# Attention and two feed-forward blocks on one core: the strided masks' queue, raw weight buffers, and the constants of the kernel's planner

## The chip, the cores and the metric

The kernel runs on one core of a Trainium2 chip. The core has a matrix engine (TensorE, PE below; PEld is its weight load), a vector engine (VectorE, DVE), an activation engine (ScalarE, ACT), GpSimd (POOL) and a sync engine (SyncE, SP) that only issues DMAs. Time is device microseconds of one execution; three runs of the kernel before took 823.49, 823.75 and 825.63 us, median 823.75 us.

## The reference, cut to what matters

```python
# attention: 4 batches, 8 heads, 576 positions, 64 per head
scores = scale * np.matmul(q, k.transpose(0, 1, 3, 2))
mask_local   = (rel >= 0) & (rel < 32)                       # heads 0 to 3
mask_strided = (rel >= 0) & (pos_k % 32 == pos_q % 32)       # heads 4 to 7
scores = np.where(mask, scores, -1e9)
attn = softmax(scores)                                       # exp, sum + 1e-9, divide
x = np.matmul(attn, v)                                       # gathered to 2304 tokens x 512
# first feed-forward block
h = x @ w_in;  g = h * np.clip(h + 3.0, 0.0, 6.0) / 6.0;  x = g @ w_out      # 512 -> 2048 -> 512
# second
h = x @ w_in2; g = h * np.tanh(softplus(h));              out = g @ w_out2
```

## The kernel before

**Layout and precision.** The host reorders q, k and v by pairs of heads (4 pairs a batch: 0 and 1 local, 2 and 3 strided), and hands the weights over as 64-bit words. `unpack` loads one 128x512 half of a weight block (a tile `raw`, 512 KB, L793), turns it into float32 in `wa` by four or five DVE instructions, one of them on ACT for the first 20 tiles (the magnitude, L797; then L807, L811, L816, L822 or L830). `split` (L348, L776) writes a float32 tile as a rounded high part (a CAST, mostly on ACT) and a low part (a subtraction on DVE or POOL). A product of two such tiles is three matmuls (`mm3`, L1012 to L1014).

**Stages.** The first feed-forward block begins before attention has ended. Its first part takes four of sixteen blocks of the hidden width plainly, in five runs of tokens (512, 448, 512, 320, 512), while batches 1 to 3 go through attention. The rest of it and the whole second block take 384 tokens twice at a time by a seven-product (Strassen-like) scheme, whose sums and differences of weights (`difference`, L898), of x (L958) and of g (L1237, L1255) run on DVE or POOL, and whose results are added up on DVE (L1221, L1295).

**Attention of one pair** (`attend`): a group of 76 score matmuls (L609), three mask additions on DVE (L622), row maximum (L654), subtraction (L655, DVE or POOL), exp on ACT (L656), row sum (L657), a guard (L661 or L663), reciprocal (L666), multiplication (L667, DVE or POOL), six transposes on PE (L676, L678), copies of them out of PSUM (`pt`, L348), 72 value matmuls (L715), and two copies into `xs`. The first two pairs take the softmax in two halves of 320 and 256 columns. `load_pair` loads q and k of a pair (`qk`, 576 KB), the values (`v`, 432 KB and a small rest) and copies some of their rows (L575, on ACT mostly). The tiles of pairs 2 and 3 of batch 0 lie in the `xs` tiles, so their loads and copies read `xs<-in_qkv_dram`.

**Masks.** The local mask comes in one load (`mk`, L489). The strided one comes in seven small loads of rows of 64 floats (`mk_str`, `mk_odd`, L515), issued by ACT with a due time of 1000, and POOL or DVE then place parts of them (L532).

**Order.** Nothing is ordered by hand. `Plan` holds every operation with costs by engine, dependencies and a due time; `run` lays them out in time with the constants at the head of the file, takes for each engine the most urgent operation that can start soonest (within `SOON`), and, where an operation may run on several engines, the one that would end it first, after a `BIAS` for each. Where PE would be idle in the first 60 us it puts in matmuls on zeros (`fill`, L1382; 'fillers' below), whose result nobody reads. The order in which `run` laid them out is the order of each engine's instructions in the program; each engine takes its own strictly in that order, and an instruction waits for the semaphores of what it needs.

**DMA semaphores.** The DMAs of all queues take eight semaphores in turn (DMAHW0 to DMAHW7). A DMA whose semaphore is taken is issued only after the transfer eight DMAs before it has landed. The planner before does not count this.

**Buffers.** There are two `raw` tiles. The load of a third waits until the first has been decoded.

## Time and profile before

| what | value |
|---|---|
| three runs | 823.49, 823.75, 825.63 us |
| the profiled execution | 822.89 us |
| its span (first to last instruction) | 821.10 us |
| mean granted clock of TensorE | 0.997 of full |
| busy: PE, DVE, ACT, POOL | 808.3, 676.0, 447.2, 325.9 us |
| DMA | 182.31 MB, mean 222 GB/s |
| last PE instruction ends | 3.4 us before the end of the span |

The page gives one profiled execution. Its time (822.89 us) holds 1.79 us that lie outside the span, and is 0.86 us under the median of the three runs. PE busy includes the fillers, so a busy PE in the first 60 us is not always at work for the result. The idle time of an engine is put down to what ended it.

### The profile page before, as it was taken

Reading aid. Unit: us, or ns where it says so; the run is one execution under the profiler, and the core shown is the slowest. Engines: PE = TensorE matmul, PEld = TensorE weight load, DVE = VectorE, ACT = ScalarE, POOL = GpSimd, SP = SyncE. Lnnn points to the kernel's source line nnn. Section 1 sums busy time; section 2 is a strip of 40 time slices with the busy share of each in tenths; the row PEclk is TensorE's granted clock in tenths of the full one; section 3 lists DMA queues with packets and bytes.
Section 4 is the critical chain, followed back from the end, with each engine's and each line's share of the span. In section 5 each row is a group of like instructions: output and inputs, shape, how many; then the busy total and the mean of one; then the engine's idle time right before and its main releaser. Section 6 shows DMA issues by size and latency. Waiting matters only on the chain.

```text
span 821.1 us, 17043 instructions
## 1 busy us (share of the span) xinstructions
PE 808.3 (98%) x6650; PEld 771.0 (94%) x6650; DVE 676.0 (82%) x1238; ACT 447.2 (54%) x941; POOL 325.9 (40%) x324
## 2 busy tenths in 40 slices
PE   6999999999999999999999999999999999999998
PEld 3678888899999999999999999999999999999998
DVE  4888887898999857867889899776888999998766
ACT  2767767666654434434436568556555545545542
POOL 4443421412252314231424324422677456476223
PEclk9999999999999999999999999999999999999999
DMA  8786751477678866765866446665667667765732
GB/s 241 229 248 184 211 178 54 146 303 268 249 251 297 295 251 238 263 226 184 288 219 229 184 168 268 225 239 196 241 240 244 225 212 244 247 237 188 246 126 96
DMA packets 47588, 182.31 MB, mean 222 GB/s; under 512 B 6036, under 2 KB 15380, under 8 KB 47508
## 3 DMA queue, kind: packets, MB, share of 16 engines
q1 hardware_dynamic: 46848, 181.06, 64.0%
q8 instruction: 52, 0.85, 0.4%
q10 hardware_dynamic: 660, 0.16, 0.1%
q14 instruction: 28, 0.23, 0.1%
HBM read 138.74 MB, written 42.47 MB: 221 GB/s over the span
## 4 chain that ended last, share of the span: by engine, by line
PE 89%; DVE 4%; DMA 3%; ACT 1%; POOL 1%; issue 1%; ACTq 0%; SPq 0%; DVEq 0%
PE bank L1012 29%; PE bank L1013 28%; PE bank L1014 28%; PE bank L715 2%; DMA raw<-in_wts_dram 1%; PE bank L609 1%; DMA v<-in_qkv_dram 1%; PE bank L676 1%; DMA mk_str<-in_masks_dram 1%; POOL w L898 1%; PE bank L1382 0%; DMA qk<-in_qkv_dram 0%; DVE wa L816 0%; DVE xs L1295 0%; DVE wa L811 0%
## 5 line engine op out<-in xcount | busy, mean ns | idle before, releaser
L1012 PE MATMUL bank<-x,win 128*128 128x384 f32 (+3 forms) x668 | 227.8, 341 | 0.4 <-POOL win L776 0.2
L1013 PE MATMUL bank<-x,win 128*128 128x384 f32 (+3 forms) x668 | 226.2, 339 | 0.1
L1014 PE MATMUL bank<-x,win 128*128 128x384 f32 (+3 forms) x668 | 226.1, 338 | 0.0
L1012 PE MATMUL bank<-g,wout 128*128 128x384 f32 (+3 forms) x512 | 175.7, 343 | 0.0
L1013 PE MATMUL bank<-g,wout 128*128 128x384 f32 (+3 forms) x512 | 174.2, 340 | 1.1 <-DVE g L776 1.1
L1014 PE MATMUL bank<-g,wout 128*128 128x384 f32 (+3 forms) x512 | 174.0, 340 | 0.0
L1295 DVE TENSOR_TENSOR xs<-bank,xs 128x384 f32<-128x384 f32 x174 | 95.2, 552 | 49.5 <-PE bank L1014 48.3
L1012 PEld LDWEIGHTS bank<-x,win 128*128 128x128 f32 x668 | 125.4, 188 | 5.3 <-POOL win L776 1.4
L1013 PEld LDWEIGHTS bank<-x,win 128*128 128x128 f32 x668 | 125.4, 188 | 2.8 <-POOL x L776 0.5
L1014 PEld LDWEIGHTS bank<-x,win 128*128 128x128 f32 x668 | 125.4, 188 | 2.2
L1013 PEld LDWEIGHTS bank<-g,wout 128*128 128x128 f32 x512 | 96.1, 188 | 3.0 <-DVE g L776 1.1
L1014 PEld LDWEIGHTS bank<-g,wout 128*128 128x128 f32 x512 | 96.1, 188 | 2.3
L1012 PEld LDWEIGHTS bank<-g,wout 128*128 128x128 f32 x512 | 96.1, 188 | 2.0
L898 POOL TENSOR_TENSOR w<-w 128x256 f32<-128x256 f32 x80 | 68.2, 871 | 70.1 <-DVE w L830 69.0
L1013 PE MATMUL bank<-g_late,wout 128*128 128x384 f32 x204 | 68.1, 334 | 0.0
L1012 PE MATMUL bank<-g_late,wout 128*128 128x384 f32 x204 | 68.1, 334 | 0.0
L1014 PE MATMUL bank<-g_late,wout 128*128 128x384 f32 x204 | 68.1, 334 | 0.0
L776 POOL TENSOR_TENSOR x<-xs,x 128x512 fp32r<-128x512 f32 (+3 forms) x17 | 21.1, 1244 | 63.7 <-ACT x L348 52.9
L816 DVE SCALAR_TENSOR_TENSOR wa<-raw,wa 128x512 uint32<-128x512 uint32 x64 | 45.8, 723 | 0.3
L776 POOL TENSOR_TENSOR win<-w,win 128x256 fp32r<-128x256 f32 (+1 forms) x25 | 29.1, 1170 | 40.6 <-ACT win L348 34.9
L348 ACT CAST win<-w 128x512 fp32r<-128x512 f32 (+1 forms) x56 | 31.6, 567 | 22.8 <-DVE w L830 14.6
L348 ACT COPY u<-bank 128x384 f32<-128x384 f32 x42 | 20.2, 482 | 37.6 <-PE bank L1014 37.4
(139 smaller groups left out, 1481.6 us busy)
## 6 DMA issues: line engine op xcount, KB each, us to landing
x<-kept_s SPq DMA_DIRECT2D x60, 768.0 KB, 4.4
x<-kept_a SPq DMA_DIRECT2D x45, 768.0 KB, 4.6
raw<-in_wts_dram SPq DMA_DIRECT2D x64, 512.0 KB, 5.0
kept_s<-x SPq DMA_DIRECT2D x24, 768.0 KB, 3.4
kept_a<-x SPq DMA_DIRECT2D x18, 768.0 KB, 4.0
qk<-in_qkv_dram SPq DMA_DIRECT2D x14, 576.0 KB, 5.3
v<-in_qkv_dram SPq DMA_DIRECT2D x14, 432.0 KB, 5.0
keep<-y SPq DMA_DIRECT2D x24, 192.0 KB, 4.1
```

What stands on the lines that cost most here:

```text
L348: nc.scalar.copy(out, src)
L609: nc.tensor.matmul(banks[both[h].n][g * QN:(g + 1) * QN, slot * WK:(slot + 1) * WK], src.q[h * D:(h + 1) * D, n // 6, n % 2 * QN:(n % 2 + ...
L676: nc.tensor.transpose(banks[turned[0].n][:, j * P:(j + 1) * P], e[:, t:t + 2].rearrange("p s k -> p (s k)"), ident)
L715: nc.tensor.matmul(o[h * D:(h + 1) * D], src.v[rows, NB + others(local).index(n) if n in others(local) else i, h * D:(h + 1) * D], pt[rows ...
L776: lambda eng: engines[eng].tensor_tensor(lo(), src(), hi().bitcast(F32), ALU.subtract),
L816: lambda: nc.vector.scalar_tensor_tensor(ai, high, 0xC0000000, ai, ALU.bitwise_and, ALU.bitwise_or),
L898: lambda eng: engines[eng].tensor_tensor(of[out], of[x], of[y], ALU.subtract), [*on[x], *on[y]], lock=("dve", "pool"),
L1012: nc.tensor.matmul(o, low_w, high, start=first, stop=False, skip_group_check=True)
L1013: nc.tensor.matmul(o, high_w, low, start=False, stop=False, skip_group_check=True)
L1014: nc.tensor.matmul(o, high_w, high, start=False, stop=last, skip_group_check=True)
L1295: "dve", dve_ns(n), lambda: nc.vector.tensor_tensor(y(), src(), y(), ALU.add), [prev, y_sums[key]], due=due, frees=frees,
```

## The change

The seven loads of the strided masks go to the sync queue and get a due time of 14000. Three more `raw` tiles, allocated beside attention's, serve with the two old ones for the first eight weight loads; the end of attention's memory then waits for their decoding too. `run` now lets a DMA start only once the eighth before it has landed (`LANES`). And most constants of the planner get new values, which moves instructions on all engines. Over the whole program the order has 1356 DVE instructions after 1240 (116 more), POOL 204 after 329, ACT's 945 after 943 beside its DMAs, and 18 fillers of 512 columns after 17; of the 80 weight differences on POOL (L898) 54 go to DVE.

```diff
+N_RAW_MORE, RAW_EARLY = 3, 8
+LANES = 8
-START, FIRST_PACE = 42920, 3359
+START, FIRST_PACE = 40873, 3220
-MASKS_DUE = 1000
-SOON = 11
+MASKS_DUE = 14000
+SOON = 0
-BIAS = {"act": -305, "dve": 318, "pool": 0}
+BIAS = {"act": -834, "dve": 384, "pool": 290}
...
                     if e == "pe":
                         t += self.late(t, op)
+                    elif e == "dma" and len(landed) >= LANES:
+                        t = max(t, landed[-LANES])
...
+            if e == "dma":
+                landed.append(op.end + self.AFTER[e])
...
+    raw_t.extend(ap_.tile([P, DM], U64, name=f"raw_more{k}") for k in range(N_RAW_MORE))
...
-            return add("act", 430, lambda: nc.scalar.dma_start(to(rows), src), due=MASKS_DUE)
+            return add("dma", 400, lambda: nc.sync.dma_start(to(rows), src), due=MASKS_DUE)
...
-        raw, a = raw_t[n % N_RAW], wa_t[n % N_WA]
+        slot = n % (N_RAW + N_RAW_MORE) if n < RAW_EARLY else n % N_RAW
+        raw, a = raw_t[slot], wa_t[n % N_WA]
...
-        old = raw_ops[n - N_RAW] if n >= N_RAW else []
+        old = raw_last.get(slot, [])
...
+            if slot >= N_RAW:
+                closing.deps.append(o)
```

Line numbers of the kernel after are 5 to 11 higher than those of the kernel before (L609 becomes L615, L1012 becomes L1023).

**The sync queue at the start.** The rows are the DMAs that SP issues, in order, with the semaphores that each waits for. `mk` is the local mask, `qk0`, `qk1`, `xs0` and `xs1` hold q and k of pairs 0 to 3, `v0` and `v1` the values of pairs 0 and 1. Before:

```order
L489 DMA mk_139<-in_masks_dram 128x320
L547 DMA qk0_143<-in_qkv_dram 128x1152
L547 DMA qk1_144<-in_qkv_dram 128x1152
L547 DMA xs0_75<-in_qkv_dram 128x1152 [waits DMAHW2_49]
L559 DMA v0_145<-in_qkv_dram 96x1152 [waits DMAHW3_49]
L547 DMA xs1_76<-in_qkv_dram 128x1152 [waits DMAHW4_49]
L559 DMA v0_145<-in_qkv_dram 64x128 [waits DMAHW5_49]
L793 DMA raw0_79<-in_wts_dram 128x512 [waits DMAHW6_49]
L559 DMA v1_146<-in_qkv_dram 96x1152 [waits DMAHW7_49]
L559 DMA v1_146<-in_qkv_dram 64x128 [waits DMAHW0_49]
L559 DMA xs2_77<-in_qkv_dram 96x1152 [waits DMAHW1_49]
L793 DMA raw1_80<-in_wts_dram 128x512 [waits DMAHW2_49]
```

And now:

```order
L497 DMA mk_139<-in_masks_dram 128x320
L800 DMA raw0_79<-in_wts_dram 128x512
L553 DMA qk0_143<-in_qkv_dram 128x1152
L800 DMA raw1_80<-in_wts_dram 128x512
L553 DMA qk1_144<-in_qkv_dram 128x1152
L553 DMA xs0_75<-in_qkv_dram 128x1152
L523 DMA mk_str_141<-in_masks_dram 128x1x64 x2
L523 DMA mk_odd_142<-in_masks_dram 64x1x64 [waits DMAHW0_49]
...
L523 DMA mk_str_141<-in_masks_dram 64x1x64 [waits DMAHW4_49]
L565 DMA v0_145<-in_qkv_dram 96x1152 [waits DMAHW5_49]
L553 DMA xs1_76<-in_qkv_dram 128x1152 [waits DMAHW6_49]
L565 DMA v0_145<-in_qkv_dram 64x128 [waits DMAHW7_49]
```

Two raw loads move to the front, the seven mask loads stand behind `xs0`, and the wait for `xs0`'s own landing (DMAHW5) now stands before the load of the first values.

**ACT at the start.** `wa` is a weight tile being decoded, `e0` and `e1` the scores of pairs 0 and 1, `pt0` the transposed ones. Before:

```order
L1381 ACT_TABLE_LOAD
L1381 ACTIVATE scratch_161<-xs0_75 128x1
L656 ACTIVATE e0_147<-e0_147 128x320
L575 COPY v0_145<-v0_145 32x1024
L656 ACTIVATE e0_147<-e0_147 128x256
L661 ACTIVATE sum0_155<-sum0_155 128x5
```

Now:

```order
L1392 ACT_TABLE_LOAD
L1392 ACTIVATE scratch_161<-xs0_75 128x1
L804 ACTIVATE wa0_81<-raw0_79 128x512
L355 CAST win0_69<-wa0_81 128x512
L804 ACTIVATE wa1_82<-raw1_80 128x512
L662 ACTIVATE e0_147<-e0_147 128x320
L662 ACTIVATE e0_147<-e0_147 128x256
L667 ACTIVATE sum0_155<-sum0_155 128x5
L667 ACTIVATE sum0_155<-sum0_155 128x4
L355 CAST wout0_71<-wa1_82 128x512
L581 COPY v0_145<-v0_145 32x1024
```

Both halves of the first exp now stand before the copy that waits for the values' load, and two weight tiles are decoded before or between them.

**PE around its last filler.** `e0` and `e1` are here the scores of pairs 0 and 1 of batch 1; x, win are the first product's operands, g, wout the second's. Before:

```order
L1012 MATMUL bank1_62<-x_73,win0_69 128x512
L1013 MATMUL bank1_62<-x_73,win0_69 128x512
L1014 MATMUL bank1_62<-x_73,win0_69 128x512
L1382 MATMUL bank5_66<-xs0_75 128x512
L1382 MATMUL bank6_67<-xs0_75 128x512
L676 MATMUL bank0_61<-mk_139,e1_148 128x128 x4
L678 MATMUL bank3_64<-mk_139,e1_148 128x128 x2
L609 MATMUL bank2_63<-qk1_144 32x64
```

Now:

```order
L1025 MATMUL bank1_62<-x_73,win0_69 128x512
L1393 MATMUL bank5_66<-xs0_75 128x512
L1393 MATMUL bank7_68<-xs0_75 128x512
L682 MATMUL bank2_63<-mk_139,e0_147 128x128 x4
L684 MATMUL bank0_61<-mk_139,e0_147 128x128 x2
L1023 MATMUL bank6_67<-g_74,wout0_71 128x512
L1024 MATMUL bank6_67<-g_74,wout0_71 128x512
L1025 MATMUL bank6_67<-g_74,wout0_71 128x512
L721 MATMUL bank0_61<-pt0_159,v0_145 64x32 x2
```

Before, the last filler stands ahead of the transposes of batch 1's pair 1; now it stands ahead of those of pair 0, and behind it come a first matmul group of the second product, pair 0's values and (not shown) six matmuls with `win1`, before the transposes of pair 1.

## Rows read from the trace of the kernel before

**Rows 1.** The page: busy time by engine, and the chain by engine.

```profile
PE 808.3 (98%) x6650; PEld 771.0 (94%) x6650; DVE 676.0 (82%) x1238; ACT 447.2 (54%) x941; POOL 325.9 (40%) x324
PE 89%; DVE 4%; DMA 3%; ACT 1%; POOL 1%; issue 1%; ACTq 0%; SPq 0%; DVEq 0%
```

**Rows 2.** Stretches: length; PE, PEld, DVE, ACT, POOL busy (count); granted clock; DMA share; GB/s.

```profile
10.00:20.00 10.00, 6.58 (x165) 3.94 (x164) 3.97 (x13) 3.24 (x11) 5.43 (x16) 0.91 1.04 277
30.00:40.00 10.00, 9.89 (x241) 6.05 (x240) 9.97 (x18) 7.61 (x14) 4.58 (x4) 1.00 0.79 243
300.00:400.00 100.00, 100.00 (x579) 100.00 (x578) 76.97 (x144) 41.61 (x85) 33.32 (x34) 1.00 0.68 238
600.00:700.00 100.00, 100.00 (x578) 100.00 (x578) 93.73 (x157) 52.56 (x112) 62.06 (x57) 1.00 0.67 233
```

**Rows 3.** Timeline of PE: start, us, line, out<-in, count, idle before.

```profile
5.72 1.05 PE L609 MATMUL bank<-qk 64*32 64x64 f32 x76 [0.77 <-DMA qk<-in_qkv_dram]
7.42 1.05 PE L609 MATMUL bank<-qk 64*32 64x64 f32 x76 [0.65 <-DMA qk<-in_qkv_dram]
19.00 4.04 PE L1382 MATMUL bank<-xs 128*128 128x512 f32 x6
22.98 1.25 PE L715 MATMUL bank<-pt,v 64*64 64x32 f32 x72
30.76 0.39 PE L1013 MATMUL bank<-x,win 128*128 128x512 f32 x1
30.99 0.40 PE L1014 MATMUL bank<-x,win 128*128 128x512 f32 x1
49.82 0.66 PE L676 MATMUL bank<-mk,e 128*128 128x128 f32 x4 [0.34 <-POOL e L667]
```

**Rows 4.** Timeline of SP's issues.

```profile
1.19 0.97 SPq L547 DMA_DIRECT2D qk<-in_qkv_dram  x2
7.08 0.33 SPq L547 DMA_DIRECT2D xs<-in_qkv_dram  x1
26.91 0.33 SPq L793 DMA_DIRECT2D raw<-in_wts_dram  x1
```

**Rows 5.** Timeline of ACT.

```profile
14.45 1.04 ACT L575 COPY v<-v 32x1024 f32<-32x1024 f32 x1 [4.58 <-DMA v<-in_qkv_dram]
20.25 0.67 ACT L797 ACTIVATE wa<-raw 128x512 f32<-128x512 f32 x1
```

**Rows 6.** Timeline of DVE.

```profile
7.03 1.07 DVE L622 SCALAR_TENSOR_TENSOR e<-bank,mk_loc 128x320 f32<-128x320 f32 x3 [3.25 <-PE bank L609]
9.90 0.49 DVE L657 TENSOR_REDUCE sum<-e 128x5 f32<-128x320 f32 x1
10.30 0.80 DVE L654 TENSOR_REDUCE nmax<-e 128x5 f32<-128x320 f32 x2
15.97 0.42 DVE L657 TENSOR_REDUCE sum<-e 128x4 f32<-128x256 f32 x1 [4.86 <-ACT e L656]
22.32 0.41 DVE L811 TENSOR_SCALAR wa<-wa 128x512 uint32<-128x512 uint32 x1
23.69 0.68 DVE L816 SCALAR_TENSOR_TENSOR wa<-raw,wa 128x512 uint32<-128x512 uint32 x1
26.76 0.75 DVE L667 TENSOR_TENSOR e<-e,sum 128x576 f32<-128x576 f32 x1
```

**Rows 7.** Groups by line and shape: count, busy us, mean ns, idle before.

```profile
L776 DVE TENSOR_TENSOR x<-f,x 128x384 fp32r<-128x384 f32 x34 | 19.2, 593 | 1.8 <-ACT x L348 1.7
L898 POOL TENSOR_TENSOR w<-w 128x256 f32<-128x256 f32 x80 | 68.2, 871 | 70.1 <-DVE w L830 69.0
```

**Rows 8.** The chain that ended last, in order of time: start, us, what.

```profile
7.45 6.98 DMA v<-in_qkv_dram
263.83 1.45 POOL w L898 x2
743.63 2.97 POOL w L898 x3
```

## The prediction

> **What bounds the kernel now.** I read the page first. PE is busy 98% of the span and carries 89% of the chain that ended last; DVE follows with 82% [rows 1]. Then the stretches: from 300 to 400 us and from 600 to 700 us PE is busy all of the time at full clock [rows 2]. Its matmuls there are the same in both kernels, so the change can't make those stretches shorter; it can move the point where PE becomes full, and it can make or remove waits afterwards. So I read the start, engine by engine. In it PE does little for the result: from 10 to 20 us it is busy 6.58 of 10 us, and part of that is fillers [rows 2].

> Why it is so empty stands in four rows. SP issues the first two loads of q and k by 2.16 us, and its next only at 7.08 us [rows 4]: that load waits for the semaphore of a mask load, one of the seven that ACT put into the ring of eight. The first values are behind it, issued at 7.45 us and 6.98 us under way [rows 8]. ACT stands 4.58 us at the copy of these values [rows 5], with the second half of the first exp queued behind that copy, and DVE idles 4.86 us for this exp [rows 6]. [...] The third raw load waits for a decoded buffer until 26.91 us [rows 4]. From 30 to 40 us DVE is the bound, busy 9.97 of 10 us [rows 2].

> **The change part by part: the start.** I walk the new order by durations of the old trace.

> Landings. The second q and k load lands 1.70 us after the first (7.42 against 5.72, where the scores start [rows 3]), 590 KB at 347 GB/s; the stretch from 10 to 20 us runs at 277 GB/s [rows 2]. Now 524 KB of raw weights stand ahead of each of the first two: +1.5 and +3.0 us. Scores 0 can start about 7, scores 1 about 10.3, and `xs0` lands about 12. That is a loss of 1.3 and 2.9 us, and in the same time DVE gets weights to decode: ACT's 0.67 [rows 5], then two times 0.41 and two times 0.68 us [rows 6] for each tile. The first tile ends near 8.0 us, when the first mask addition is ready.

> DVE from there. Up to the multiplication of batch 1's pair 1 the new order has 82 instructions: 7 triples of mask additions at 1.07 us, 8 wide reductions, 8 wide subtractions or multiplications and 2 in halves, taken as 18 at 0.75, 8 half reductions as 4 at 0.80, 10 of the 0.41 and 9 of the 0.68 us kind for weights, 6 of 512 columns at 0.68 us, 11 small ones at some 0.2 us [rows 6]. Sum: 7.5 + 13.5 + 3.2 + 4.1 + 6.1 + 4.1 + 2.2 = 40.7 us. Each starts some 0.07 us before the recorded end of the one before (9.90 + 0.49 against 10.30 [rows 6]), so 82 of them take 35 us. From 8.0 us that gives 43; waits for the second scores (1.1 us), for exp behind the `pt` copies (0.7) and for ACT's casts and guards (1.4) bring it to 46.2 us.

> PE at that point. Ahead of these transposes its order now has a filler, the transposes of pair 0, three matmuls of the second product, pair 0's values and six matmuls with `win1`. Pair 0's multiplication ends near 38.4 us on the same walk, but the filler and the two groups before it hold its transposes to about 43.2. With 0.9 + 0.7 + 1.25 + 1.4 us of work the transposes of pair 1 follow at 47.5 us. In the old trace they start at 49.82 us [rows 3]: 2.3 us earlier, and nine matmuls at 0.23 us (start to start, 30.76 to 30.99 [rows 3]), 2.1 us, are done that were still to do. Lead: 4.4 us.

> I take 1.1 us off it. Two more raw tiles, 1.05 MB, now come before the second batch's q, k and v, 3.8 us at 277 GB/s; the bubble of 4.9 us on SP (2.16 to 7.08) pays for these, but not for the new wait: the first values are now issued only when `xs0` has landed, since seven of eight semaphores are taken by the masks. ACT's copy of batch 1's first values is where the walk is tight, about a microsecond. The lead is thus **3.3 us**, with 0 and 5.5 us as its ends: none if the transfers set the pace throughout, 5.5 if landings keep 347 GB/s and the filler costs nothing.

> Seven issues leave ACT and cost SP some 0.5 us each (two took 0.97 [rows 4]), 3.5 us that lie beside the 8 us in which its loads queue anyway. I cost them at nothing; if SP were late, 3.5 us would come off the lead. [...]

> **After the start.** 116 instructions come to DVE. None of the weight differences ran there; POOL's took 871 ns, a DVE subtraction over 384 columns 593 ns [rows 7]. For 256 columns I take 0.4, near the latter by size, and 0.47 on average of all: 55 us in all, less what DVE gains because fewer POOL instructions run beside it. That gain shows between two stretches: from 300 to 400 us a DVE instruction takes 76.97/144 = 0.535 us with 34 of POOL's beside, from 600 to 700 us 93.73/157 = 0.597 us with 57 [rows 2]; the mixes differ, but as it stands 0.062 × 157 / 23 = 0.42 us for each POOL instruction. So the busiest 100 us get some 25 instructions, +11.7 and −10.5 us, and DVE stays near 95%. I cost it at nothing. Its gain: two of the chain's pieces off PE are POOL's differences, 1.45 and 2.97 us long [rows 8], behind which PE waited under a microsecond each; DVE would do them in half the time. Ends for all waits after the start: 2.5 us less, 7 us more (below). I take zero, since at 82% DVE has room and the old waits are short.

> **The sum.** Profiled execution 822.89 us − 3.3 = 819.6 us. The median of the runs is 0.86 us above it, so 823.75 − 3.3 = **820.4 us**.

> **Rivals.**

> *The transfers set the pace, and nothing is gained.* For it: DMA is at 1.04 of its share from 10 to 20 us, 277 GB/s [rows 2], more bytes come forward, and scores 1 start 2.9 us later. The lead of DVE's decoding is then waited away at batch 1's loads. Against it: the old queue stood still twice, for 4.9 us and until 26.91 us [rows 4], and both go. Time: lead 0 to 1.5 us, 822.3 to 823.8; about 823.2.

> *DVE becomes the bound of the second block; slower.* Its place is the stretch from about 585 to 710 us, where DVE is at 93.73% [rows 2]. If the instructions moved to it cost 0.47 us and nothing is returned, it needs 105.4 us in 100, over 125 us 6.8 us more than PE: 823.75 − 3.3 + 6.8 = 827.2 us. It decides from a return below 0.22 us per POOL instruction taken away. [...]

> *The lead is kept, and the short chains of weights remove the later waits too.* 823.75 − 5.5 − 2.5 = 815.8 us at best; about 817.5.

> **How the numbers follow.** Forecast (818.5 to 822) 0.46; transfers 0.24; slower DVE 0.16; better still 0.14. The range is 816.5 to 826.0 us: it leaves out some of the best case and of the slower one, and the likeliest case's own is 818.5 to 822. A measurement tells about 0.3% (2.5 us) from no change, so faster means below 821.3. From the forecast four fifths lie there, and all of the best case: 0.37 + 0.14 + a little of the transfers' case, 0.52; slower (above 826.2) 0.13 of the slow case's 0.16; the rest, 0.35, is within.

> **What would show it.** Right: ACT's first idle time is for raw weights and not for values; the transposes of batch 1's pair 1 start near 47.5 us with nine more matmuls of the products behind them; from 300 us on PE is as full as before; DVE's busy time rises by some 5 to 30 us and POOL's falls by a third. Wrong: scores 1 or `xs0` much later than 10.3 and 12 us; PE idle at "raw" or "qk" between 25 and 45 us; PE waiting for DVE by more than 3 us in all after 200 us.

## The result and the profile after: 828.5 us, slower

The changed kernel takes 828.48 us (median of 5 runs, 827.37 to 832.71) where the kernel before takes 823.75 us (5 runs, 823.33 to 825.63); the ratio is 1.0055, with a 95% interval of 1.0032 to 1.0079. The forecast was 820.4 us, and the range ended at 826.0. The profiled execution took 828.72 us, its span 826.9 us. Engines and chain of its page answer to [rows 1]:

```profile
PE 813.0 (98%) x6652; PEld 773.5 (94%) x6652; DVE 705.8 (85%) x1354; ACT 450.1 (54%) x950; POOL 214.1 (26%) x199
PE 93%; DVE 4%; ACT 1%; issue 1%; DMA 1%; SPq 0%; DVEq 0%
```

PE is busy 4.7 us longer with two instructions more, ACT has nine more (950 after 941), and PE's share of the chain rose. The stretches of the profile after, in the columns of [rows 2]:

```profile
10.00:20.00 10.00, 9.55 (x205) 5.03 (x205) 8.24 (x21) 3.53 (x8) 7.00 (x16) 1.00 0.81 224
25.00:30.00 5.00, 2.05 (x73) 1.51 (x72) 4.14 (x6) 2.45 (x8) 1.42 (x1) 0.79 1.07 268
30.00:40.00 10.00, 9.68 (x245) 7.66 (x244) 6.98 (x13) 6.97 (x16) 1.28 (x1) 0.76 0.96 278
40.00:45.00 5.00, 3.07 (x7) 1.36 (x8) 4.55 (x11) 2.98 (x6) 0.00 (x0) 0.66 0.36 93
300.00:400.00 100.00, 100.00 (x578) 100.00 (x578) 77.33 (x154) 40.05 (x82) 16.14 (x15) 1.00 0.68 238
600.00:700.00 100.00, 100.00 (x579) 100.00 (x578) 95.01 (x182) 52.92 (x115) 42.64 (x37) 1.00 0.67 232
```

To 20 us DVE is twice as busy as in [rows 2], as it was meant to be. PE is at 9.55 of 10 us, but 6.51 of that are fillers (3.10 of its 6.58 us before): by work for the result it was no fuller. From 25 to 30 us PE does 2.05 of 5 us. From 300 us on PE is as full as before. PE's timeline shows where it stands, and how it runs behind that (what answers to [rows 3]: start, us, line, count, idle before and its cause):

```profile
6.87 1.19 PE L615 MATMUL bank<-qk 64*32 64x64 f32 x76
10.76 1.18 PE L615 MATMUL bank<-qk 64*32 64x64 f32 x76
...
25.67 1.12 PE L721 MATMUL bank<-pt,v 64*64 64x32 f32 x60 [0.30 <-ACT pt L355]
29.44 0.64 PE L721 MATMUL bank<-pt,v 64*64 64x32 f32 x12 [2.65 <-issue]
...
31.58 1.40 PE L615 MATMUL bank<-qk 64*32 64x64 f32 x76
32.91 1.11 PE L682 MATMUL bank<-mk,e 128*128 128x128 f32 x4
...
36.67 1.25 PE L721 MATMUL bank<-pt,xs 64*64 64x32 f32 x72
37.85 0.66 PE L682 MATMUL bank<-mk,e 128*128 128x128 f32 x4
38.65 1.02 PE L615 MATMUL bank<-qk 64*32 64x64 f32 x72
41.93 0.43 PE L615 MATMUL bank<-qk 64*32 64x64 f32 x4 [2.26 <-issue]
42.29 3.31 PE L1393 MATMUL bank<-xs 128*128 128x512 f32 x4
...
57.22 0.60 PE L682 MATMUL bank<-mk,e 128*128 128x128 f32 x4
```

Twice PE stops in the middle of a group, with 12 of 72 and 4 of 76 matmuls left, for 2.65 and 2.26 us, and the profile names no engine and no transfer: "issue". In each stop the granted clock falls to 0.5 and stays there from 27.9 to 34.8 us and from 41.6 to 45.0 us: the same four transposes take 1.11 and then 0.66 us, and four filler instructions 3.31 us. The last row is the place that the prediction walked to: 57.22 us instead of 47.5.

The lag of the changed kernel at equal work of PE (both lists of matmuls without fillers, each at its full-clock duration, added up and compared) gives the place of the loss. A minus means that the kernel is ahead. The last two columns are experiments below:

```
time before, us   lag after   e8_paced   e13_paced_moved
  26.6              -0.3         0.7          0.2
  31.7               3.0         0.9          1.2
  42.0               5.3         2.9         -0.4
  55.7               3.7         1.3         -1.8
  83.8               6.8         4.0          0.7
 368.6               7.9         4.8          1.5
 817.4               5.9         2.9         -0.5
```

All of the loss arises between 26 and 84 us. From there to the end the changed kernel loses 1.1 and wins back 2.0 us. It arises in two places: to 42 us, where the two stops lie, and again by some 3 us from 55.7 to 83.8 us. The second loss is in the two other columns too (2.7 and 2.5 us), so the experiments below do not touch it.

### The profile page after: what moved, and what is told of

Same layout as the page of the kernel before. It is cut to its first block, busy times and chain, and to the rows that moved or that the text cites. A ratio compares the mean times of both kernels' runs of the same rounds, so it can differ in the third digit from the quotient of the medians.

```text
span 826.9 us, 17024 instructions
## 1 busy us (share of the span) xinstructions
PE 813.0 (98%) x6652; PEld 773.5 (94%) x6652; DVE 705.8 (85%) x1354; ACT 450.1 (54%) x950; POOL 214.1 (26%) x199
## 4 chain that ended last, share of the span: by engine, by line
PE 93%; DVE 4%; ACT 1%; issue 1%; DMA 1%; SPq 0%; DVEq 0%
PE bank L1023 29%; PE bank L1025 28%; PE bank L1024 28%; PE bank L721 2%; PE bank L1393 2%; PE bank L615 2%; DMA v<-in_qkv_dram 1%; PE bank L682 1%; DVE u L1157 0%; DVE xs L1296 0%; PE bank L684 0%; DVE v L1157 0%; DVE wa L814 0%; DVE e L628 0%; ACT v L581 0%
## 5 line engine op out<-in xcount | busy, mean ns | idle before, releaser
L1023 PE MATMUL bank<-x,win 128*128 128x384 f32 (+3 forms) x668 | 229.4, 343 | 1.3 <-DVE t L1157 1.1
L1023 PE MATMUL bank<-g,wout 128*128 128x384 f32 (+3 forms) x512 | 175.1, 342 | 0.0
L1023 PEld LDWEIGHTS bank<-x,win 128*128 128x128 f32 x668 | 125.6, 188 | 5.3 <-issue 1.4
L1023 PEld LDWEIGHTS bank<-g,wout 128*128 128x128 f32 x512 | 96.1, 188 | 1.9
L1023 PE MATMUL bank<-g_late,wout 128*128 128x384 f32 x204 | 68.1, 334 | 0.0
L823 DVE SCALAR_TENSOR_TENSOR wa<-raw,wa 128x512 uint32<-128x512 uint32 x60 | 41.5, 695 | 0.5
L355 ACT COPY v<-bank 128x384 f32<-128x384 f32 x42 | 20.1, 478 | 38.8 <-PE bank L1025 38.5
L355 ACT CAST g<-t 128x384 fp32r<-128x384 f32 (+3 forms) x60 | 32.0, 535 | 12.7 <-DVE t L1157 5.1
L1024 PEld LDWEIGHTS bank<-g_late,wout 128*128 128x128 f32 x204 | 38.3, 188 | 0.0
L1025 PEld LDWEIGHTS bank<-g_late,wout 128*128 128x128 f32 x204 | 38.3, 188 | 0.0
```

Source lines behind the costliest of these rows:

```text
L355: nc.scalar.copy(out, src)
L823: lambda: nc.vector.scalar_tensor_tensor(ai, high, 0xC0000000, ai, ALU.bitwise_and, ALU.bitwise_or),
L1023: nc.tensor.matmul(o, low_w, high, start=first, stop=False, skip_group_check=True)
L1024: nc.tensor.matmul(o, high_w, low, start=False, stop=False, skip_group_check=True)
L1025: nc.tensor.matmul(o, high_w, high, start=False, stop=last, skip_group_check=True)
```

## Experiments: one part at a time

Two theories stood at the start. *Supply*: PE gets its instructions in blocks over the same DMA engines as the data (the page after counts 52 packets of the kind `instruction`, 0.85 MB, 0.4% of the 16 engines' span); the raw weights that are now loaded early hold them up. *Constants*: the refitted numbers of the planner gave a worse order. (A third, that the masks on SP's queue delay what is behind them, is told apart by the same runs.) The first four kernels each undo or do one part, and the planner then orders everything anew.

**The new structure with the old numbers:**

```diff
-START, FIRST_PACE = 40873, 3220
+START, FIRST_PACE = 42920, 3359
...
-BIAS = {"act": -834, "dve": 384, "pool": 290}
+BIAS = {"act": -305, "dve": 318, "pool": 0}
```

> The structure of the changed kernel (masks on the sync queue, three more raw buffers, eight transfers counted) with the old constants of the planner. Supply theory: PE loses the start because its instructions come in blocks over the same DMA engines as the data, and the raw weights loaded early keep these engines full; those loads are still there, so PE waits for 'issue' by 2 us or more in all between 20 and 60 us, and the time is 825 to 829 us. Constants theory: the refitted constants gave a worse order; with the old ones 821 to 824 us.

Measured: 833.98 us, ratio 1.0118 (1.0099 to 1.0138). **The kernel before with the new numbers alone** (the reverse edit):

> The kernel before (masks on ACT's queue, two raw buffers) with the new constants alone. Supply theory: with two raw buffers little comes early, the waits for 'issue' in the first 60 us stay at about the 1.0 us of before or below 1.5 us, and the time is 821 to 825 us. Constants theory: 827 to 830 us, as the changed kernel.

Measured: 833.85 us, ratio 1.0118 (1.0097 to 1.0139). **Two raw buffers:**

```diff
-N_RAW_MORE, RAW_EARLY = 3, 8
+N_RAW_MORE, RAW_EARLY = 0, 8
```

> The changed kernel with two raw buffers instead of five; masks on the sync queue, new constants. Supply theory: 1.6 MB less are loaded ahead of the second and third pair's work, the waits for 'issue' between 20 and 60 us fall from 5.1 us to under 2 us, and the time is 822 to 825 us. If the masks on the sync queue, or the constants, cost the time: 827 to 830 us.

Measured: 836.91 us, ratio 1.0146 (1.0117 to 1.0175). **Masks back on ACT:**

```diff
-return add("dma", 400, lambda: nc.sync.dma_start(to(rows), src), due=MASKS_DUE)
+return add("act", 430, lambda: nc.scalar.dma_start(to(rows), src), due=MASKS_DUE)
...
-MASKS_DUE = 14000
+MASKS_DUE = 1000
```

> The changed kernel with the strided masks back on ACT's queue, due at once; five raw buffers, new constants. Supply theory: the raw loads are still there, waits for 'issue' of 2 us or more, 825 to 830 us. If it is the masks on the sync queue that delay the rest: 821 to 824 us.

Measured: 832.20 us, ratio 1.0100 (1.0080 to 1.0121). Every one is slower than both kernels and than every range that was expected, so no part can be called the cause from their times: each time the planner writes another order. Their waits say more. Some of those of PE in the first 100 us (line, cause: us in all, times, longest), of the kernel before with the new numbers:

```profile
PE bank L609 <- issue: 3.3, 2, 1.9
PE bank L609 <- DMA qk<-in_qkv_dram: 2.7, 2, 1.6
PE bank L715 <- issue: 0.9, 1, 0.9
```

and of the kernel with two raw buffers:

```profile
PE bank L721 <- issue: 3.5, 1, 3.5
PE bank L615 <- DMA qk<-in_qkv_dram: 2.3, 1, 2.3
```

The supply theory said under 1.5 and under 2 us there. It falls in the form in which I had it: the additional raw buffers are not needed for these waits. The constants theory falls too, since the old numbers gave 833.98 us. What these four kernels share is PE waiting for "issue" for 4.3 to 5.1 us in the first 100 us (the changed one: 5.4); the kernel before has 1.0 us of it:

```profile
PE bank L715 <- issue: 1.0, 1, 1.0
```

## Experiments: what the waits are

The trace has a record of each block: 16 KB, 52 of them in the span of the changed kernel, for 13,451 records of PE (13,304 matmuls and weight loads, the rest almost all semaphore instructions), so some 256 instructions each. The planner holds that a block is asked for when PE is at place 140 + 256k of its stream, and begins at 448 + 256k, 308 instructions later (`PIECE`, `ASKED`, `AHEAD`). For each block I read when PE passed the first place, when the block's transfer began (the delay), and how long PE took for the 308 instructions. From that beginning to PE's next instruction it is 2.7 us (26.72 to 29.44 and 39.19 to 41.93 in the profile after). So a wait should be delay + 2.7 − time for the 308. The wait seen is taken from start to start of the two instructions around it; the idle time in the profile's rows is some 0.2 us less:

```
kernel, block         asked at  delay  308 instr  formula  wait seen
before, third           19.01    5.67    8.01        0.36     0.33
before, eighth          46.41    5.44    6.78        1.36     1.17
after, third            20.34    6.38    6.23        2.84     2.87
after, fifth            35.42    3.77    4.04        2.44     2.47
e5_shift, third         25.49    5.11    4.00        3.82     3.94
e6_small_raw, third     20.22    4.58    5.94        1.33     1.23
e8_paced, third         21.65    3.55    5.94        0.30     0.43
e8_paced, fifth         33.25    3.72    4.02        2.40     2.12
e10_extra_load, third   17.37    7.53    8.04        2.19     2.29
e13, third              21.22    4.75    5.91        1.55     1.39
e13, fifth              33.66    3.46    5.67        0.49     0.27
```

Over the first ten blocks of all 16 kernels, 160 blocks, the formula gives more than 1 us 28 times; the wait seen is then off by 0.13 us on average (0.45 at most). 96 times it gives less than −0.3 us, and no step from start to start there is longer than 0.53 us. The place of asking cancels out of the formula, which therefore tests only that PE goes on 2.7 us after a block's transfer began. For the place speaks something else: of all 833 blocks in the 16 traces none began sooner than 0.86 us after PE passed it, while 177 began before PE was 20 instructions further. The planner of both kernels takes 6.0 us from asking to having (`SUPPLY`); the third block after took 9.1.

The next kernels keep the whole order of the changed kernel. **The stream shifted by half a block:**

```diff
...
+        if first:
+            first.clear()
+            for _ in range(33):
+                nc.tensor.matmul(banks[n][:32, :64], zeros[:64, :32], zeros[:64, :64], start=True, stop=True)
+            return
...
```

> The changed kernel; the first of the fillers that run before any data are there is replaced by 33 tiny matmuls, so that every later instruction of PE stands 128 places further back in the instruction stream (half a block). All orders and transfers stay. Supply theory: the waits for 'issue' belong to places in the stream (about 960 and 1472), not to work. They leave the value matmuls of pair 1 (place 960 before, now 1088) and the end of the scores (1472, now 1600); the first shows 128 instructions earlier in the work, at the transposes of pair 1 near 24 us, and is 3 to 5 us long, because PE now takes only 4.3 us for the 308 instructions ahead of it and the block comes 6.4 + 2.7 us after it is asked for. Time 826 to 831 us. If the waits belong to the work itself (a semaphore that the profile does not show, a slow operand), they stay at the value matmuls and the scores, of 2.65 and 2.26 us.

Measured: 830.76 us, ratio 1.0089 (1.0064 to 1.0113). PE's timeline of this kernel:

```profile
28.98 0.38 PE L682 MATMUL bank<-mk,e 128*128 128x128 f32 x2
29.20 0.27 PE L684 MATMUL bank<-mk,e 128*128 128x128 f32 x1
29.33 0.44 PE L682 MATMUL bank<-mk,e 128*128 128x128 f32 x2
33.44 0.33 PE L684 MATMUL bank<-mk,e 128*128 128x128 f32 x1 [3.67 <-issue]
```

The wait left the value matmuls and stands 128 instructions earlier in the work, in the transposes; the one in the scores is gone. The waits belong to places in the stream. **Fewer data in the way:**

```diff
+        w = DM // 16 if n in (2, 3, 4) else DM
...
-        load = add("dma", dma_ns(8 * P * DM), lambda: nc.sync.dma_start(raw, wts[m, f, half]), old)
+        load = add("dma", dma_ns(8 * P * DM), lambda: nc.sync.dma_start(raw[:, :w], wts[m, f, half][:, :w]), old)
...
```

> The changed kernel with the first three loads into the additional raw buffers (the third to fifth raw weight tile) cut to a sixteenth of their columns, so wrong weights come out; all orders stay. 1.5 MB, 6 us of transfers at 247 GB/s, go away between 17 and 35 us. Supply theory: instruction blocks queue behind the data that are outstanding when they are asked for; with less ahead of them the delays of the third and fifth block (6.38 and 3.77 us) fall by 1.5 to 3 us, the waits for 'issue' of 5.1 us fall to under 1.5 us, the granted clock stays up, and the time is 821 to 824.5 us. If it is not the transfers that hold up the blocks, the waits stay at 4 us or more and the time at 827 to 829 us.

Measured: 825.47 us, ratio 1.0022 (1.0008 to 1.0035). These three tiles then hold wrong weights. The third block's delay fell by 1.8 us, as expected; the fifth's stayed at 3.79, and with it the second wait; the time stayed above the 821 to 824.5 us of the theory:

```profile
PE bank L615 <- issue: 2.1, 1, 2.1
PE bank L721 <- issue: 1.0, 1, 1.0
```

**Fillers inside the waits** (three ahead of the value matmuls, four ahead of the scores):

```diff
+FILL_AT = {23: 3, 32: 4}
...
+                for _ in range(FILL_AT.get(turn, 0)):
+                    plan.filler[2](op.banks[0].n if op.banks else 2)
```

> The changed kernel with seven more fillers on PE, which cost 6.0 us of its time at full clock: three ahead of the value matmuls of pair 1 (in which it waits 2.65 us) and four ahead of the scores in which it waits 2.26 us. All else in its order. Supply theory: PE waits for the block with or without them, so they run inside the time of the waits, which shrink to under 1 us in all; and since PE does not stand still, its granted clock stays up behind them, which gives back 2 to 3.5 us: 825 to 827 us. If the waits have another cause, or the half-speed stretches are not due to PE's standing still, the fillers come on top: 830 to 834 us.

Measured: 831.87 us, ratio 1.0102 (1.0061 to 1.0143): a miss. In its trace the second block came late (delay 6.14 us), so PE waited 1.39 us at 25 us already, one block earlier, and the fillers ran on top. That trace is of the slowest of four executions (835.83; the others 827.83 to 832.50 us). It does not tell what the half clock costs. **At most three large loads outstanding** (`paced` stands around the loads of q and k, v and raw weights):

```diff
+    def paced(ins):
+        n = len(big)
+        if 7 <= n < 19:
+            info = mybir.DependencyInfo(mybir.DependencyClass.Sync, mybir.DependencyReason.DATA)
+            tc.add_manual_dep(ins.ins, big[n - 3].name, info, reason="paced")
+        big.append(ins.ins)
...
```

> The changed kernel; each of twelve large loads between 12 and 36 us also waits until the third large load before it has landed, so that at most three are outstanding. No byte and no order changes. Supply theory: landings are set by the rate and stay within 1 us, while blocks that are asked for find less ahead of them: delays of the third to fifth block 1 to 2 us shorter, waits for 'issue' of 5.1 us down to 1.5 to 3.5 us, time 823 to 827 us. If outstanding transfers do not matter for the blocks: no change of the waits, and 828 to 831 us where loads come later.

Measured: 825.95 us, ratio 1.0028 (1.0010 to 1.0046). The delays of the third to fifth block are 3.55, 4.03 and 3.72 us (6.38, 7.89, 3.77 before the edit): the first wait shrinks to 0.21 us, the second does not. That data came sooner is not the reason: from 10 us on PE waits for no load in either kernel, and ACT waits for loads for 1.8 us in the changed kernel and 2.2 us in this one (10 to 70 us).

```profile
28.02 0.42 PE L730 MATMUL bank<-pt,v 64*64 64x32 f32 x12 [0.21 <-issue]
...
39.40 0.32 PE L624 MATMUL bank<-qk 64*32 64x64 f32 x4 [1.91 <-issue]
39.65 2.87 PE L1402 MATMUL bank<-xs 128*128 128x512 f32 x4
42.44 1.95 PE L730 MATMUL bank<-pt,xs 64*64 64x32 f32 x72
```

Its granted clock is 1.00 from 25 to 35 us, behind the wait of 0.21 us, and 0.66 from 40 to 45 us, behind that of 1.91 us. **One load more held back:**

```diff
-            tc.add_manual_dep(ins.ins, big[n - 3].name, info, reason="paced")
+            tc.add_manual_dep(ins.ins, big[n - (2 if n == 15 else 3)].name, info, reason="paced")
```

> As the run with at most three large loads outstanding, and the first value load of the second batch waits for one load more, so that it is issued after PE asks for its fifth block (33.25 us there) and not before it. Supply theory: that block's delay falls from 3.72 to 1.5 to 2.5 us, its wait of 1.9 us to under 0.8 us, and the fall of the granted clock behind it goes too (2 us): 821.5 to 824 us, 2 to 4 us under the run before. If the last wait has another cause, it stays at 1.9 us and the time at 825 to 827 us.

Measured: 824.89 us, ratio 1.0028 (1.0010 to 1.0046); the medians alone give 1.0008, since the times of this kernel spread with its clock (last section). A miss: the delay stayed at 3.75 us, although only 66 GB/s moved from 32.5 to 34 us. Loads issued before the block was asked for (32.13 us) therefore do not explain what is left. The load held back was issued 0.44 us behind the asking, and landed at 35.6 to 36.7 us, just as the block came (35.9); whether the block waited for that one the run does not tell, and what makes the rest stays open (other blocks came after 0.9 us). **The opposite dose, in the kernel before:**

```diff
...
+            if k == 4:
+                nc.sync.dma_start(unused, wts[0, 0, 0])
...
```

> The kernel before, with one more load of 512 KB, of weights that nobody reads, issued behind the load of q and k near 15 us; all orders stay. Supply theory: PE's third block, asked for at 19.0 us, finds 2.1 us more ahead of it (5.67 becomes about 7.8 us), PE reaches its end 8.0 us after asking and waits for 'issue' by about 2.4 us (0.33 now) at the value matmuls near 27 us; its clock then falls for some microseconds; 826 to 829 us. If outstanding data do not hold up the blocks: no wait for 'issue' over 0.5 us there, and 823 to 825 us (up to 826 if the loads behind it come late).

Measured: 824.14 us, ratio 1.0003 (0.9990 to 1.0016). The delay rose to 7.53 us and the wait to 2.29, as expected, but not the time. In this trace PE was 1.6 us ahead of the profiled execution of before at 26.6 us (it waited 0.9 us for `xs`, 2.5 before), 1.3 us behind after the wait, and 1.9 us behind at the end; the medians of the two kernels show none of it. Why is open, and with it whether such waits must cost time in every kernel. PE's waits in this trace:

```profile
PE bank L722 <- issue: 4.5, 3, 2.1
```

**The planner told 9.0 us** (`SUPPLY = 9000`):

> The changed kernel with one number of its planner changed: a block of instructions is taken to come 9.0 us after it is asked for, instead of 6.0 us, which is what the trace of the changed kernel shows for its third block (6.38 + 2.7). The whole order is planned anew. Supply theory: the waits for 'issue' in the first 60 us fall from 5.1 to under 2.5 us; the time is less sure, since the order is new: 823 to 830 us. If the waits are not to be planned away: 4 us or more, over 828 us.

Measured: 840.93 us, ratio 1.0204 (1.0179 to 1.0230), a miss, with 3.8 us of "issue" still: another order, worse, and a constant does not describe a delay that went from 0.9 to 8.7 us among blocks asked for between 15 and 33 us.

## Experiments: the second wait, and both together

Ahead of the second wait PE has values, transposes and scores in a row: 308 small instructions in 4.0 us, and two fillers directly behind. **The fillers (PE's turns 33 and 34 in the plan) moved ahead of the scores (turn 32):**

```diff
+            if op.engine == "pe" and turn in (33, 34):
+                continue
+            if op.engine == "pe" and turn == 32:
+                for _ in range(2):
+                    plan.filler[2](op.banks[0].n)
```

> The changed kernel; the two fillers that stand on PE behind the scores in which it waits 2.26 us now stand ahead of these scores. Nothing is added. If the order of PE makes this wait: PE takes 1.7 us more for the 308 instructions ahead of the block's end, the wait shrinks from 2.26 to about 0.5 us, and the value matmuls behind the scores start up to 2.5 us earlier; the wait at the value matmuls near 27 us stays: 826 to 827.5 us, 1 to 2.5 us under the changed kernel. If the wait has another cause, it stays and the scores are late by the fillers: 828 to 830.5 us.

Measured: 826.76 us, ratio 1.0032 (1.0020 to 1.0043). The first wait stayed (2.38 us), the second is 0.59 us:

```profile
40.23 1.88 PE L1393 MATMUL bank<-xs 128*128 128x512 f32 x4
43.55 0.33 PE L615 MATMUL bank<-qk 64*32 64x64 f32 x8 [0.59 <-issue]
43.82 1.25 PE L721 MATMUL bank<-pt,xs 64*64 64x32 f32 x72
```

**Both edits:**

> At most three large loads outstanding, as before, and the two fillers moved ahead of the scores. If outstanding data make the first wait and the order of PE the second: both are under 0.6 us, the granted clock stays up from 20 us on, and the time is 823 to 824.5 us, 1.5 to 3 us under the run with three loads outstanding alone. If not: 825.5 to 827 us.

Measured: 823.34 us, ratio 0.9994 (0.9980 to 1.0008). Its first wait is 1.17 us (a delay of 4.75 us in this run, 3.55 in the run with pacing alone), the second is gone. The theory had both under 0.6 us and the clock up; the granted clock fell to 0.5 from 29.7 to 33.1 us, behind the first:

```profile
28.51 0.42 PE L730 MATMUL bank<-pt,v 64*64 64x32 f32 x12 [1.17 <-issue]
...
36.80 1.88 PE L1402 MATMUL bank<-xs 128*128 128x512 f32 x4
38.62 1.32 PE L624 MATMUL bank<-qk 64*32 64x64 f32 x76
39.86 1.25 PE L730 MATMUL bank<-pt,xs 64*64 64x32 f32 x72
...
51.79 0.60 PE L691 MATMUL bank<-mk,e 128*128 128x128 f32 x4
```

**And three groups of dense matmuls moved behind the transposes** (`turn` 27 to 29 emitted after 30):

> As the run before, and the three groups of dense matmuls of the second product that stand ahead of the values in front of these scores now stand behind their transposes. The 308 instructions then take PE about 7 us instead of 4.0, more than the 3.7 + 2.7 us that the block takes; no wait for 'issue' over 0.3 us there: 822.5 to 824.5 us. If the transposes' inputs are late instead, DVE or ACT ends PE's waits there: 824 to 826 us.

Measured: 824.35 us, ratio 1.0008 (0.9994 to 1.0022). The second wait is gone here too (PE takes 6.75 us for the 308), and the first is 0.42 us; the waits for `pt` went from 0.6 to 1.4 us. The time is no shorter than with both edits. No version here is faster than the kernel before; the changed one is brought back to it, 0.6% faster than it was.

## Why the prediction was wrong

**The step that failed** is the walk that gave "Lead: 4.4 us": DVE's and PE's work was laid end to end, and PE's own instructions were taken to be there: their supply stands in no term of the sum, although the planner in the kernel reckons with it. At its end, the transposes of batch 1's pair 1, the kernel before stands at 49.82 us [rows 3], or 51.9 with the nine matmuls; after is at 57.22, so the lead of 4.4 us is a lag of 5.3. With the two repairs it is 51.79, no lead and no lag. So, by these single traces, 5.4 of the 9.7 us of error at this place went with the two edits that act on the supply; the other 4.3 us are what the walk had too short. That run still holds a wait of 1.17 us, a granted clock of 0.69 from 30 to 35 us, and its first scores at 7.9 instead of 7 us; the runs do not divide the 4.3 us further. Two slips in the walk do not explain them: its list has 83 instructions, not 82, and the overlap in its row is 0.09 us (10.39 against 10.30), not 0.07, which would make it 1.7 us shorter still.

How a wait of PE spread is in the rows of ACT and DVE after (the first two follow on the first wait, one behind the other; the last follows on the second wait):

```profile
29.93 0.72 ACT L355 COPY xs<-bank 128x288 f32<-128x288 f32 x2 [2.50 <-PE bank L721]
```

```profile
31.85 1.35 DVE L782 TENSOR_TENSOR win<-wa,win 128x512 fp32r<-128x512 f32 x1 [2.71 <-ACT win L355]
48.20 0.69 DVE L782 TENSOR_TENSOR x<-xs,x 128x512 fp32r<-128x512 f32 x1 [2.84 <-ACT x L355]
```

The two DVE rows alone are 5.5 us; the walk had 3.2 us for all of DVE's waits. With both repairs the same two waits are 0.8 and 0.2 us.

**The sum by ratios.** After is 1.0055 of before, 1.0028 with three loads outstanding, 1.0032 with the fillers moved, 0.9994 with both: 2.2, 1.9 and 5.0 us of 823.75. Alone, neither edit is clear of noise against the changed kernel (the intervals overlap); both together are: 5.0 us, give or take 2.3 by the two intervals. The forecast asked for 0.9959. So of 7.9 us of error 5.0 went with PE's supply and the fall of its clock behind a wait, which the runs do not divide, and 2.9 are lead that was not there at the end. With both repairs PE is 1.8 us ahead at 55.7 us, some 1.0 of it because the kernel before waits for a block of its own there, and it has lost 2.5 us by 83.8 us. 1.0 us of this loss is one wait of its scores for a mask addition on DVE, which is busy 5.00 of 5 us there (60 to 65 us); the rest is open.

**What held.** Scores 0 and 1 start at 6.87 and 10.76 us (7 and 10.3 forecast). ACT's first long idle time is for raw weights. From 300 us on PE is as full as before. DVE's busy time rose by 29.8 us (5 to 30 forecast), POOL's fell by 34% (a third). `xs0` landed at 10.93 us (about 12 forecast), and the first two mask loads, issued behind it, at 10.98 and 11.44 us. The weight differences of 256 columns on DVE, unseen before and taken at 0.4 us, take 0.48 (871 ns on POOL [rows 7]):

```profile
L909 DVE TENSOR_TENSOR w<-w 128x256 f32<-128x256 f32 x54 | 24.6, 480 | 0.2
```

The term "after the start, 0" came to +0.6 us by the lag (5.3 us at the walk's last place, 5.9 at the end), but by luck: −1.6 to 55.7 us, where the kernel before has its own wait for a block, then the +3.1 to 83.8 us, and then +1.1 and −2.0. *Rivals.* DVE as the bound of the second block did not come: 95.01 of 100 us there (near 95 forecast), with PE at 100.00. The transfers did set the pace, but not as that rival had it: PE waited for no load of data in the first 100 us; the blocks of its instructions between them were late. The range was too narrow since no case and no sign of being wrong looked at PE's wait of 0.96 us for "issue" at 54 us, which the trace of before shows: the margin that it tells of is what the change uses up.

## What to carry to other kernels

Look for "issue" in PE's waits, however small (1.0 us in the first 100 us of the kernel before): where PE has long rows of small matmuls, find how long it takes for some 300 instructions and compare that with how long a block of instructions takes to come while loads are outstanding (the fifth block after: 308 in 4.04 us against 3.77 + 2.7 us). The change started loads earlier and packed small matmuls tighter, and so used up this margin (the 308 instructions up to the third block took 6.23 us instead of 8.01) with PE waiting for no load of data in the first 100 us. Two cheap repairs, which were clear of noise only together: do not issue loads long before they can flow (with three outstanding 256 GB/s flowed from 12 to 36 us, 268 without the edit), and put fillers inside the tight row, not behind it (the second wait went from 2.26 to 0.59 us).
